# An attention and two-MLP kernel: half-height first score products, one cast moved to ScalarE, result stores on GpSimd's queue, and new planner numbers

## The chip, the cores and the metric

The kernel runs on one core of one Trainium2 chip. The metric is device time in microseconds (us), the median of several runs. Engines are named as the profile names them: PE (TensorE; PEld is its weight load), DVE (VectorE), ACT (ScalarE), POOL (GpSimd) and SP (SyncE, which here only issues transfers; "SPq" and "POOLq" are the queues on which these two engines issue DMAs).

## The reference

```python
scores = np.matmul(z, z.transpose(0, 2, 1)) / S          # B=2, S=3008, z is 64 wide
out = np.matmul(np.maximum(scores, 0.0) ** 2, v)
x = (u * out).reshape(B * S, 256)                         # attention result
h = x @ w_in                                              # first MLP, 256 -> 2048
g = (a0 + a1*h + a2*h**2 + a3*h**3) / (1 + |b0|*|h| + |b1|*h**2 + 1e-6)
x = g @ w_out                                             # 2048 -> 256
h = x @ w2_in                                             # second MLP
g = np.maximum(h, 0.0) + alpha * np.minimum(h, 0.0)
result = g @ w2_out
```

The weights arrive as 64-bit floats and are taken apart on the chip.

## The kernel before, in words

All products are made in a reduced 32-bit format, so each operand is split into a high half (a cast) and a low half (the original less the cast), and a product is two or three matmuls. The attention runs over 12 blocks (2 batches of 6 blocks of 512 queries, the last 448 wide) with 12 pairs of key tiles each. A score tile goes PE (`L912`) -> ACT (relu `L927`/`L935`, square `L940`, cast `ahi` `L463`) -> DVE (`alo` `L468`) -> PE (8 products `L963` with `ahi`, 4 products `L974` with `alo`). Score tiles are symmetric, so DVE also transposes some (`L824`), SP writes them to DRAM (`rt<-rt`) and reads them back for a later block (`rr<-rt`). At the end of a block (`a_end`) SP loads `ut`, DVE multiplies the accumulators with it (`L1007`), and the result goes to DRAM (`xd`, `L1013`), from where the first MLP reads it (`xr`, `L1064`).

Beside the attention DVE, ACT and POOL decode the 32 pieces of the weights (`weight`, tiles `wraw` and `dec`, DVE lines `L576` to `L657`), and the first 17 steps of the first MLP run. A step of the first MLP is 12 products (`L1034` to `L1036` into `h`), seven DVE operations (`L1093` to `L1105`) that make `ghi` and `glo`, and 12 products back (`L963`, `L974`). The second MLP has its hidden products into `m` or `h` and two DVE operations (`L1163`, `L468`) for each step.

No scheduler of the compiler is used. Every instruction is recorded as an operation of `Plan` with an assumed duration, and `Plan.order()` plays these through with a cost model: an engine takes the ready operation with the earliest due time, buffers come from numbered rooms, and the resulting order is written out. Each engine then works strictly in its order. The order of PE is the order of recording. The constants at the top (`PACE`, `SAME`, `SOONER`, `SAFE`, `AFTER`, `NEXT`, `DEBT`, `EDGE`, `R0`, `RD`, `SOON`, `FAR`) are the costs, horizons and pacing of this planner: `AFTER` and `SAFE` are how long after its issue a transfer is taken to land, `R0` and `RD` say at which attention steps the weight pieces are recorded, and `DEBT` and `EDGE` how much DVE work may be outstanding when one more is recorded. `WARM` is the number of matmuls on zeros before the first real one.

In the opening `load_z` makes `zA`: rows 0 to 63 hold the high half of z (the cast), rows 64 to 127 the low half (`L709`). `zB` has the halves the other way round. A score is `zA·zA` plus `zB·zA`. For the very first tile the two products are recorded apart, so that the first can run before `zB` is there.

## Time and profile before

| | |
|---|---|
| median of 3 runs | 1495.2 us (1494.6 to 1495.29) |
| the profiled execution's own time | 1494.43 us |
| its span, first to last instruction | 1492.6 us |
| PE busy | 1484.3 us, 99% |
| DVE busy | 1413.4 us, 95% |
| ACT busy | 1182.2 us, 79% |
| POOL busy | 80.8 us, 5% |

The span is what the trace covers; 1.8 us of the execution lie outside it. Shares are of the span. PE is busy almost throughout, so the time is the sum of PE's products and of the few places in which PE stands.

### The profile page before, as it was taken

The numbers are of one execution on the slowest core, as the hardware profiler recorded it, in microseconds if no ns is written. First come the engines' busy times: TensorE is split into PE (matmuls) and PEld (weight loads), VectorE is DVE, ScalarE is ACT, GpSimd is POOL, SyncE is SP. The second block draws the span as 40 slices with busy tenths as digits, with TensorE's granted clock in tenths as the row PEclk, the third lists the DMA queues.
The fourth block names the chain that finished last, engine by engine and source line by source line (L and its number), as shares of the span: only waits on it lengthen the run. The fifth ranks groups of instructions, "written<-read, shape, count | busy, mean of one in ns | idle before, by whom it ended". The sixth has DMA issues, their size and how long they took to land.

```text
span 1492.6 us, 18002 instructions
## 1 busy us (share of the span) xinstructions
PE 1484.3 (99%) x6655; PEld 1242.4 (83%) x6655; DVE 1413.4 (95%) x1459; ACT 1182.2 (79%) x1403; POOL 80.8 (5%) x98
## 2 busy tenths in 40 slices
PE   9999999999999999999999999999999999999999
PEld 7888888888887888888888888888888888888988
DVE  8899999999999999999999999989999999999953
ACT  8888868887877868797788778778887888788844
POOL 1000000011122330000000000000000000000000
PEclk9999999999999999999999999999999999999999
DMA  6998677668996863000000000000000000000000
GB/s 199 236 247 212 192 212 237 160 164 230 251 263 214 288 224 123 19 29 15 29 29 29 29 14 29 15 29 29 29 29 14 29 15 29 29 25 29 15 1 25
DMA packets 195145, 149.77 MB, mean 100 GB/s; under 512 B 154336, under 2 KB 166128, under 8 KB 195056
## 3 DMA queue, kind: packets, MB, share of 16 engines
q1 hardware_dynamic: 185424, 114.00, 27.6%
q0 software_dynamic: 9632, 34.62, 7.1%
q8 instruction: 52, 0.85, 0.2%
q14 instruction: 37, 0.30, 0.1%
HBM read 86.52 MB, written 59.24 MB: 98 GB/s over the span
## 4 chain that ended last, share of the span: by engine, by line
PE 91%; DVE 6%; issue 1%; DMA 1%; ACT 0%; DVEq 0%; ACTq 0%
PE acc L963 36%; PE acc L974 18%; PE h L1036 6%; PE h L1035 6%; PE h L1034 6%; PE m L1036 5%; PE m L1035 5%; PE m L1034 5%; PE s L912 3%; PE acc L953 1%; PE h L912 1%; DVE alo L468 1%; DVE glo L1105 0%; DMA rr<-rt 0%; DVE ghi L1102 0%
## 5 line engine op out<-in xcount | busy, mean ns | idle before, releaser
L963 PE MATMUL acc<-ghi,w 128*128 128x512 f32 (+1 forms) x1472 | 360.7, 387 | 0.0
L963 PEld LDWEIGHTS acc<-ghi,w 128*128 128x128 f32 x1472 | 275.6, 188 | 54.9
L963 PE MATMUL acc<-ahi,vt 128*128 128x512 f32 (+1 forms) x1152 | 281.1, 386 | 1.2 <-DVE ahi L856 1.0
L963 PEld LDWEIGHTS acc<-ahi,vt 128*128 128x128 f32 x1152 | 215.1, 188 | 43.0 <-DVE ahi L856 1.4
L1090 ACT ACTIVATE t<-h,sc 128x1024 f32<-128x1024 f32 (+1 forms) x96 | 114.2, 1190 | 137.8 <-PE h L1036 133.9
L974 PE MATMUL acc<-glo,w 128*128 128x512 f32 (+1 forms) x736 | 195.2, 387 | 0.4 <-DVE glo L1105 0.4
L974 PEld LDWEIGHTS acc<-glo,w 128*128 128x128 f32 x736 | 137.8, 188 | 28.4 <-DVE glo L1105 0.8
L1034 PE MATMUL h<-xhi,w 128*128 128x512 f32 (+1 forms) x412 | 157.8, 383 | 0.3 <-ACT sq L1088 0.3
L1036 PE MATMUL h<-xhi,w 128*128 128x512 f32 (+1 forms) x412 | 157.7, 383 | 0.0
L1035 PE MATMUL h<-xlo,w 128*128 128x512 f32 (+1 forms) x412 | 157.7, 383 | 0.0
L974 PE MATMUL acc<-alo,vt 128*128 128x512 f32 (+1 forms) x552 | 146.5, 385 | 0.0
L1034 PE MATMUL m<-xhi,w 128*128 128x512 f32 (+1 forms) x356 | 137.7, 387 | 1.0 <-DVE m L1163 1.0
L1035 PE MATMUL m<-xlo,w 128*128 128x512 f32 (+1 forms) x356 | 137.6, 387 | 0.0
L1036 PE MATMUL m<-xhi,w 128*128 128x512 f32 (+1 forms) x356 | 137.6, 387 | 0.0
L1157 ACT ACTIVATE m<-m,sc 128x512 f32<-128x512 f32 (+1 forms) x178 | 116.0, 693 | 22.4 <-PE m L1036 21.0
L1093 DVE SCALAR_TENSOR_TENSOR ab<-sq,cb,ab 128x1024 f32<-128x1024 f32 (+1 forms) x96 | 120.8, 1258 | 11.4 <-ACT sq L1088 11.0
L468 DVE TENSOR_TENSOR glo<-m,ghi 128x1024 fp32r<-128x1024 f32 (+1 forms) x96 | 114.8, 1196 | 10.8 <-ACT ghi L463 10.8
L1098 ACT ACTIVATE sq<-ab,one 128x1024 f32<-128x1024 f32 (+1 forms) x96 | 110.7, 1153 | 13.1 <-DVE t L1095 12.9
L974 PEld LDWEIGHTS acc<-alo,vt 128*128 128x128 f32 x552 | 103.6, 188 | 19.3
L1163 DVE TENSOR_TENSOR m<-m 128x1024 f32<-128x1024 f32 (+1 forms) x89 | 107.2, 1205 | 11.0 <-ACT m L1157 10.9
L1102 DVE TENSOR_TENSOR ghi<-t,sq 128x1024 fp32r<-128x1024 f32 (+1 forms) x96 | 114.8, 1195 | 2.5 <-ACT sq L1099 2.4
L1105 DVE TENSOR_TENSOR glo<-t,sq 128x1024 fp32r<-128x1024 f32 (+1 forms) x96 | 114.9, 1197 | 1.6
(100 smaller groups left out, 2640.1 us busy)
## 6 DMA issues: line engine op xcount, KB each, us to landing
rt<-rt SPq DMA_DIRECT2D x200, 128.0 KB, 3.6
rr<-rt SPq DMA_DIRECT2D x40, 512.0 KB, 5.6
rr<-rt SPq DMA_DIRECT2D x20, 448.0 KB, 5.9
wraw<-in_moe_w_in_dram POOLq DMA_DIRECT2D x16, 512.0 KB, 5.7
wraw<-in_moe_w_out_dram POOLq DMA_DIRECT2D x16, 512.0 KB, 5.8
wd<-dec POOLq DMA_DIRECT2D x16, 512.0 KB, 3.9
w<-wd POOLq DMA_DIRECT2D x16, 512.0 KB, 5.9
x2d<-x SPq DMA_DIRECT2D x11, 512.0 KB, 2.6
```

What stands on the lines that cost most here:

```text
L468: lambda: nc.vector.tensor_tensor(lo(), src(), hi().bitcast(F32), ALU.subtract),
L963: nc.tensor.matmul(acc()[:, e, :n], w()[:, k, i, e * P : (e + 1) * P], hi()[:, i, :n], start=first and i == 0 and k == 0, stop=False,)
L974: nc.tensor.matmul(acc()[:, e, :n], w()[:, 0, i, e * P : (e + 1) * P], lo()[:, i, :n], start=False, stop=last and i == both - 1,)
L1034: nc.tensor.matmul(acc, w_hi, hi, start=first, stop=False)
L1035: nc.tensor.matmul(acc, w_hi, lo, start=False, stop=False)
L1036: nc.tensor.matmul(acc, w_lo, hi, start=False, stop=last)
L1090: act(N, lambda: activation(c(t), c(h), AF.Identity, scale=a3, bias=a2), [h], [t], psum=True, ptr=2, **kw)
L1093: dve(N, lambda: stt(c(ab), c(sq), b1, c(ab), ALU.mult, ALU.add), [sq, ab], [ab], ptr=1, **kw)
L1098: act(N, lambda: activation(c(sq), c(ab), AF.Abs_reciprocal_sqrt, bias=one), [ab], [sq], ptr=1, **kw)
L1102: dve(N, lambda: tt(c(hi), c(t), c(sq), ALU.mult), [t, sq], [hi], **kw)
L1105: dve(N, lambda: tt(c(lo), c(t), c(sq), ALU.mult), [t, sq], [lo], **kw)
L1157: lambda i=i, f=f: nc.scalar.activation(t()[:, i, :n], h()[:, i, :n], AF.Copy, scale=al[:, f : f + 1]),
```

## The change

The first score product of the first two key pairs of block (0, 0) takes only rows 0 to 63 (high half times high half; the product of the two low halves is left out for these two pairs), and is recorded as needing only that part. The second pair's products are recorded in four pieces too. The cast of the second z group moves from DVE to ACT. The store of `xd` moves from SP's queue to GpSimd's. One matmul on zeros goes, and the planner's numbers change, so that the order on DVE, ACT, SP and POOL changes in many places.

```diff
-PACE = 25.0
-SAME = 0.16
-SOONER = 30.0
+PACE = 22
+SAME = 0.13
+SOONER = 38
 WIRE = 0.6
-SAFE = 1.0
+SAFE = 1.5
-AFTER = 4.0
-FIRST, NEXT = 5, 4
-FILL, DEBT, EDGE = 0.97, 4.0, 3.0
+AFTER = 5
+FIRST, NEXT = 5, 6
+FILL, DEBT, EDGE = 0.97, 3, 4
-R0, RD = 3, 3
-WARM = 7
+R0, RD = 1, 2.5
+WARM = 6
-NEAR, SOON, FAR = 25.0, 10.0, 40.0
+NEAR, SOON, FAR = 25.0, 12, 50
@@ load_z
-        dve(m, lambda: nc.vector.tensor_copy(t()[:, 0:m], raw()[:, 0:m]), [raw], [t], fast=True)
+        if (b, g) == (0, 1):
+            act(m, lambda: nc.scalar.copy(t()[:, 0:m], raw()[:, 0:m]), [raw], [t])
+        else:
+            dve(m, lambda: nc.vector.tensor_copy(t()[:, 0:m], raw()[:, 0:m]), [raw], [t], fast=True)
@@ load_z, zB of the first group: the two halves are recorded apart
-            act(m, lambda: nc.scalar.copy(q()[HALF:P, 0:m], raw()[HALF:P, 0:m]), [raw], [q])
+            act(m, lambda: nc.scalar.copy(q()[HALF:P, 0:m], raw()[HALF:P, 0:m]), [raw], [(q, 1)])
@@ a_scores
-                nc.tensor.matmul(o, keys, (zA, zB)[k][b, j]()[:, q0:n], start=k == 0, stop=k == 1)
-        opening = (b, j, kp) == (0, 0, 0)
+                h = slice(0, HALF if opening and k == 0 else P)
+                nc.tensor.matmul(o, keys[h], (zA, zB)[k][b, j]()[h, q0:n], start=k == 0, stop=k == 1)
+        opening = (b, j) == (0, 0) and kp in order[b, j][:2]
-                pe(n, 1, lambda i=i: mm(i, (0,)), [zk, zA[b, j]], [hs[i]])
+                pe(n, 1, lambda i=i: mm(i, (0,)), [(zk, 0), (zA[b, j], 0)], [hs[i]])
@@ a_end
-        sp(n, lambda: nc.sync.dma_start(out=d()[:, :, :n], in_=t()[:, :, :n]), [t], [d])
+        pool_dma(
+            n,
+            lambda: nc.gpsimd.dma_start(out=d()[:, :, :n], in_=t()[:, :, :n]),
+            [t], [d], level="load", rate=210.0, horizon=SOON,
+        )
```

What the change does to the order is read from the instructions of the two built programs. First DVE's opening, before (`zA` is made for three z groups in turn, `zB` for the first):

```order
L706 CAST zA<-zraw 128x512
L709 TENSOR_TENSOR zA<-zraw,zA 64x512
L706 CAST zA<-zraw 128x512
L722 TENSOR_TENSOR zB<-zraw,zA 64x512
L709 TENSOR_TENSOR zA<-zraw,zA 64x512
L706 CAST zA<-zraw 128x512
L709 TENSOR_TENSOR zA<-zraw,zA 64x512
```

and of the change (three lines lower in the file):

```order
L709 CAST zA<-zraw 128x512
L712 TENSOR_TENSOR zA<-zraw,zA 64x512
L725 TENSOR_TENSOR zB<-zraw,zA 64x512
L712 TENSOR_TENSOR zA<-zraw,zA 64x512
L709 CAST zA<-zraw 128x512
L712 TENSOR_TENSOR zA<-zraw,zA 64x512
```

The cast of the second group no longer stands ahead of `zB`. It stands on ACT, behind the cast for `zB` and ahead of the first relu.

Second, SP's queue around the first load of `ut`, before (`rt` are pieces of transposed score tiles on their way to DRAM):

```order
L871 DMA rr<-rt_0_1_100 128x1024
L838 DMA rt_0_3_102<-rt 32x16x64 x8
L838 DMA rt_0_4_103<-rt 32x16x64 x8
L998 DMA ut<-in_u_dram 128x2x512
L838 DMA rt_0_5_104<-rt 32x16x64 x4
```

and of the change:

```order
L874 DMA rr<-rt_0_1_100 128x1024
L841 DMA rt_0_3_102<-rt 32x16x64 x4
L754 DMA zB<-zA 64x512 x2
L841 DMA rt_0_3_102<-rt 32x16x64 x4
L841 DMA rt_0_4_103<-rt 32x16x64 x4
L1002 DMA ut<-in_u_dram 128x2x512
L841 DMA rt_0_4_103<-rt 32x16x64 x4
```

Between the `rr` load and the `ut` load stood 16 transfers, and now stand 14.

Third, DVE at the end of the attention, where the last `ut` multiply (448 wide) stands, before:

```order
L614 TENSOR_TENSOR dec<-dec,sr_83 128x256 x2
L603 SCALAR_TENSOR_TENSOR dec<-wraw,dec 128x512
L1095 TENSOR_TENSOR t<-t,sq 128x1024
L635 TENSOR_TENSOR dec<-dec 128x512
L608 TENSOR_TENSOR dec<-dec 128x512
L1007 TENSOR_TENSOR ut<-acc_81,ut 128x2x448
L1163 TENSOR_TENSOR m<-m 128x1024
```

and of the change (lines above `L1012` are 4 lower, those below 12):

```order
L1105 SCALAR_TENSOR_TENSOR ab<-sq,cb,ab 128x1024
L1107 TENSOR_TENSOR t<-t,sq 128x1024
L657 SCALAR_TENSOR_TENSOR dec<-dec,sg 128x256
L468 TENSOR_TENSOR xlo<-xr,xhi 128x512
L657 SCALAR_TENSOR_TENSOR dec<-dec,sg 128x256
L468 TENSOR_TENSOR xlo<-xr,xhi 128x512
L1108 TENSOR_TENSOR t<-t,c_4926 128x1024
L1011 TENSOR_TENSOR ut<-acc_81,ut 128x2x448
```

The last multiply stands further ahead, and part of the decoding that stood before it now stands behind it.

## Rows read from the trace of the kernel before

**Rows 1.** The page: busy time of each engine, share of the span, instructions.

```profile
PE 1484.3 (99%) x6655; PEld 1242.4 (83%) x6655; DVE 1413.4 (95%) x1459; ACT 1182.2 (79%) x1403; POOL 80.8 (5%) x98
```

**Rows 2.** Windows: stretch, its length, each engine's busy time (instructions), clock, DMA.

```profile
400.00:500.00 100.00, 99.00 (x440) 81.57 (x439) 96.77 (x126) 75.53 (x95) 24.52 (x24) 1.00 0.86 250
500.00:600.00 100.00, 98.19 (x446) 83.08 (x445) 99.88 (x115) 76.66 (x93) 26.30 (x30) 1.00 0.59 197
```

**Rows 3.** Waits of PE: for what, us in total, times, longest.

```profile
PE m L1034 <- DVE m L1163: 1.0, 1, 1.0
PE acc L963 <- DVE ahi L856: 1.0, 1, 1.0
PE acc L974 <- DVE glo L1105: 0.4, 1, 0.4
PE h L1034 <- ACT sq L1088: 0.3, 1, 0.3
```

**Rows 4.** Timeline of PE, 548 to 556 us: start, us, what, idle before.

```profile
548.88 0.39 PE L1036 MATMUL h<-xhi,w 128*128 128x512 f32 x1
550.32 0.50 PE L1034 MATMUL m<-xhi,w 128*128 128x512 f32 x1 [1.05 <-DVE m L1163]
550.65 0.40 PE L1035 MATMUL m<-xlo,w 128*128 128x512 f32 x1
...
555.89 0.39 PE L1034 MATMUL h<-xhi,w 128*128 128x512 f32 x1
```

**Rows 5.** Timeline of DVE, 547 to 556 us.

```profile
547.45 0.68 DVE L608 TENSOR_TENSOR dec<-dec 128x512 f32<-128x512 f32 x1
548.05 1.08 DVE L1007 TENSOR_TENSOR ut<-acc,ut 128x896 f32<-128x896 f32 x1
...
550.19 1.21 DVE L1096 TENSOR_TENSOR t<-t,c 128x1024 f32<-128x1024 f32 x1
551.32 0.47 DVE L657 SCALAR_TENSOR_TENSOR dec<-dec,sg 128x256 fp32r<-128x256 f32 x1
551.71 1.21 DVE L468 TENSOR_TENSOR glo<-m,ghi 128x1024 fp32r<-128x1024 f32 x1
...
554.38 1.28 DVE L468 TENSOR_TENSOR xlo<-xr,xhi 128x512 fp32r<-128x512 f32 x2
```

**Rows 6.** Timeline of the opening, DVE, ACT and PE.

```profile
4.71 0.43 DVE L706 CAST zA<-zraw 128x512 fp32r<-128x512 f32 x1
...
5.05 0.68 DVE L722 TENSOR_TENSOR zB<-zraw,zA 64x512 fp32r<-64x512 f32 x1
...
5.88 0.72 PE L912 MATMUL s<-zB,zA 128*128 128x512 f32 x2 [0.41 <-DVE zB L722]
...
6.40 1.09 ACT L927 ACTIVATE r<-s 128x512 f32<-128x512 f32 x2 [2.25 <-PE s L912]
```

**Rows 7.** Timeline of DVE and SP: the first load and multiply of `ut`.

```profile
40.38 13.41 SPq L838 DMA_DIRECT2D rt<-rt  x16
53.89 0.55 SPq L998 DMA_DIRECT2D ut<-in_u_dram  x1
59.43 1.22 DVE L1007 TENSOR_TENSOR ut<-acc,ut 128x1024 f32<-128x1024 f32 x1 [4.14 <-PE acc L974]
```

**Rows 8.** Timeline of PE and DVE: the fourth and the ninth multiply.

```profile
183.08 1.07 PE L974 MATMUL acc<-alo,vt 128*128 128x512 f32 x4
184.56 1.22 DVE L1007 TENSOR_TENSOR ut<-acc,ut 128x1024 f32<-128x1024 f32 x1
402.12 1.23 DVE L1007 TENSOR_TENSOR ut<-acc,ut 128x1024 f32<-128x1024 f32 x1 [1.19 <-PE acc L974]
```

**Rows 9.** Waits of SP's queue, and transfers by kind (count, KB each, us to landing).

```profile
SPq L1013 <- DVE ut L1007: 64.0, 7, 23.7
wd<-dec POOLq DMA_DIRECT2D x16, 512.0 KB, 3.9
xd<-ut SPq DMA_DIRECT2D x10, 512.0 KB, 4.3
```

More of the change, by code (lines that the diff above doesn't have):

```diff
@@ L725, in load_z @@
                 [raw, (t, 0)],
-                [q],
+                [(q, 0)],
             )
@@ L1012, in a_end @@
         xd[b, j] = d
-        sp(n, lambda: nc.sync.dma_start(out=d()[:, :, :n], in_=t()[:, :, :n]), [t], [d])
+        pool_dma(
+            n,
+            lambda: nc.gpsimd.dma_start(out=d()[:, :, :n], in_=t()[:, :, :n]),
+            [t],
+            [d],
+            level="load",
+            rate=210.0,
+            horizon=SOON,
+        )
     def split_x(src, sr, n, make, psum=False):
```

## The prediction

> **What bounds the kernel now.** I read the page first: PE is busy for 1484.3 of 1492.6 us [rows 1], so the time is PE's products plus what PE waits, and a change that alters no product's size can win at most those waits. The windows say where they are: 400:500 and 500:600 lack 1.00 and 1.81 us [rows 2]; from 600 us to the end every stretch is full. The list of PE's waits names the largest: 1.0 and 1.0 us for DVE, 0.4 for DVE and 0.3 for ACT [rows 3]. These figures are too small, because a matmul's modelled end overlaps the next start. From start to start, matmuls of 512 columns follow each other 0.23 us apart; the wait at 548.88 makes it 1.44, and the next step is 0.33 [rows 4]. So a wait that the row calls 1.05 costs 1.21 + 0.11 = 1.3 us. Taken so, the waits of [rows 3] cost 1.3, 1.3, 0.7 and 0.6 us, and what lies before them in the trace (one of 0.5 behind a `ut` multiply, four of 0.1) brings the sum to **4.8 us** between 185 and 564 us. The opening is apart: there PE stands until 5.88 us for `zB` [rows 6].
>
> The reader is then to see why PE waits: DVE is 99.88% busy in 500:600 [rows 2], and the product at 555.89 starts 0.23 us after the `xlo` that it reads has ended, the last of a stretch without gaps on DVE [rows 4, 5]. In this stretch PE's place in time is DVE's. Whatever DVE loses earlier (idle time), PE pays here.
>
> **The change, part by part.**
>
> *Opening.* With the cast of the second z group gone from DVE, `zB` follows 0.34 us earlier (4.71 to 5.05) [rows 6], the second pair of products and ACT's chain behind it (6.40 on) too. ACT has room for the cast: it is idle for 2.25 us before 6.40 [rows 6], against 0.54 us for each of the two 512-wide relus that follow. The first products can start one matmul on zeros earlier, but what follows still waits for `zB`, so the seventh is not won a second time. No row shows a matmul with 64 rows; between nothing and the 0.23 us of a full one I take the full one, since the columns are the same; the four of them then lie in the wait for `zB`, which covers them. If they cost less, that wait hides it. The part is worth **-0.34 us** where ACT's chain leads, and is contained in the DVE sum below.
>
> *DVE's work ahead of the stretch that binds.* I follow the one product at 555.89, the first of the third 512-token group of the first MLP. By the two orders, DVE has 648 instructions up to its `xlo` in both kernels: now four more of 1.13 us (`L1102`, `L1103`, `L1104`, `L1163`; as 550.19 to 551.32), one z cast of 0.34, one `L608` of 0.60 and two `L657` of 0.39 fewer [rows 5, 6]. That is 4.52 - 0.34 - 0.60 - 0.78 = **+2.8 us** ahead of it. PE has one hidden step of the second MLP more in front of it, 12 x 0.227 = 2.7 us, so 2.7 us less are left behind it. By work alone the end moves by +0.1 us: the shuffle of the order on DVE is no gain in itself.
>
> *DVE's idle time ahead of it.* Here the transfers matter.
> - First `ut`. DVE stood 4.14 us before 59.43. The row names PE, but PE's last product of the block had ended at 52.06, so it was the load, issued at 53.89 and 5.5 us on its way [rows 7]. In the new order 14 transfers instead of 16 stand between the `rr` load and this one, at 13.41/16 = 0.84 us each [rows 7]: it lands 1.7 us earlier. DVE has one transpose more and one cast fewer ahead of it (+0.8 us), so it arrives 0.8 us later. The idle time falls from 4.14 to 1.6: **-2.5 us**. Bounds: 0, if the queue is held up elsewhere, and -4.14.
> - Ninth `ut`: DVE waits 1.19 us for PE now [rows 8], and has 1.3 us more work ahead: **-1.2 us**.
> - Fourth and seventh `ut`: DVE comes 0.41 us after PE's last product at the fourth (184.56, and 183.08 + 1.07) [rows 8] and at once at the seventh. By the orders it has 1.8 and 1.5 us less work ahead, PE 0.4 less (the matmul on zeros), so DVE now waits about 1.0 us at each: **+2.0 us**. Bounds: 0 to +2.0.
> - The other gaps (waits for ACT in the middle) I take as unchanged, with 2 us either way.
>
> Sum -1.7 us. The bounds add up to -4.1 - 1.2 - 2 = -7.3 (more than PE has to give, which is rival A) and -1.2 + 2.0 + 2 = +2.8.
>
> *Behind that product.* The wait of 0.4 in [rows 3] (`L974` for `glo`, at 563.72; cost 0.7) should go: by the orders DVE has 8 us less ahead of that `glo` relative to PE. **-0.7 us.**
>
> *Stores on GpSimd's queue.* Twelve leave SP, where the queue stood 64.0 us behind this instruction in 7 waits [rows 9]; what stood behind it were `rt` and `rr` transfers, whose lateness is in the idle times above. On POOL the same wait for the multiply stands ahead of weight loads. In the order the first store stands behind two weight loads, the second and third behind six. The first reader of `xd`, a load for the first MLP, stood ten rows behind the store in SP's order, with four loads and some thirty transfers between, so the store itself costs nothing.
>
> A store by this queue is not dearer in the rows: `wd` of 512 KB lands in 3.9 us from POOL, `xd` of 512 KB in 4.3 us from SP [rows 9]. The Trainium skill speaks against it: "SBUF — State Buffer", section "SBUF: two separate sides", says that DMAs issued from GpSimd need descriptors written by GpSimd, which is locked out while DVE runs an instruction in its two-port mode, and advises SP or ACT. By that rule each store would start up to one fast DVE operation later, an estimate of 12 x 0.4 us of lateness on the queue and nothing on PE; by the rows, nothing at all. The trace does not show it.
>
> **Sum:** +0.1 - 1.7 - 0.7 = **-2.3 us**. Against the profiled execution's own 1494.43 us that is 1492.1; its span is 1492.6 with 1.8 us around it. The median of the runs stands 0.8 us above that execution, so I forecast **1492.9 us**.
>
> **The rivals.**
>
> A. *All waits go.* If DVE loses its idle time of 59.43 entirely and the fourth and seventh `ut` bring no new wait, DVE is 4 to 5 us earlier, all 4.8 us of PE's waits vanish, and the opening gives its 0.34: 1495.2 - 5.1 = 1490.1. For it speaks that lateness in this stretch has one source, that the planner now takes transfers to land 1.5 us later than before (`AFTER` and `SAFE`), so it puts fewer DVE instructions in front of data that is not there, and that the last multiply and a good part of the decoding behind it have changed places. Against it: the waits that vanish bring PE forward against a DVE that is still full.
>
> B. *Nothing moves.* The early `ut` load is held up behind another transfer (the DMA engines are busy for 0.86 of 400:500 [rows 2]), idle time only changes place, and +0.1 - 0.7 is left: 1494.6.
>
> C. *Slower.* A store that waits for its multiply on POOL holds up the weight loads behind it. SP stood up to 23.7 us behind the same instruction [rows 9]. If two weights are decoded that much later, their DVE work (seven to eight instructions each, 3.6 us from start to start by the pitches of [rows 5]) falls into 500:600, where DVE has 0.1 us free [rows 2]: +7.2 - 2.3 gives 1500. It decides against the change from 5.3 us of decoding pushed there, that is from the second late weight. Against it: the planner puts few stores ahead of loads, and POOL is busy 5% of the span [rows 1].
>
> **How the numbers follow.** My forecast (DVE 1 to 4 us earlier at 555.89, time 1491.8 to 1494.2) 0.38; A 0.33; B 0.18; C 0.11. A measurement of this kernel can tell a change of about 0.2%, 3.0 us, from none: faster is below 1492.2, slower above 1498.2. Faster: A and a small part of the forecast, 0.38. Same: the rest of the forecast and B, 0.51. Slower: C, 0.11. The range leaves out C and the far end of A: 1489.6 to 1496.8, which above 1494.6 takes in most of the +2.8 us by which DVE's idle time may grow. The likeliest case alone is 1491.8 to 1494.2.
>
> **What would show it.** In the trace after: `zB` on DVE starts near 4.7 instead of 5.05, and ACT's first relu near 6.05 instead of 6.40. The idle time before the first `ut` multiply is 1 to 2 us instead of 4.14; about 1 us stands before the fourth and the seventh. The list of PE's waits keeps one or two for DVE between 470 and 560 us, with a sum near 1.5 instead of 2.9 us, and none at the `glo` near 564. DVE stays at 99% in 500:600. The forecast is wrong if PE is full in 400:600 (then A), if the waits are as long as before (B: a DVE idle time that I took as unchanged has grown), or if POOL's weight loads come later than before and the decoding ends later (C). It is also wrong if a wait appears before 60 us, where DVE has up to 3 us more work ahead of some products and PE's margin is thin.

## The result, and the profile after

The changed kernel takes 1502.2 us (median of 4 runs, 1500.1 to 1503.6), the kernel before 1494.9 in the same session: ratio 1.0051 [1.0038, 1.0063], **slower by 0.5%**, 7.3 us. The forecast was 1492.9 with a range up to 1496.8.

The busy line of the page after answers to [rows 1]:

```profile
PE 1489.6 (99%) x6654; PEld 1243.9 (83%) x6654; DVE 1411.4 (94%) x1458; ACT 1182.7 (79%) x1405; POOL 87.9 (6%) x110
```

DVE and ACT did the same work as before to within 2 us. PE is "busy" for 5 us longer with one instruction fewer: some of its matmuls took longer. The span grew from 1492.6 to 1500.1 us. PE's waits after, against [rows 3] (for what, us in total, times, longest):

```profile
PE acc L967 <- DVE ut L1011: 2.3, 2, 1.8
PE s L455 <- DVE one L437: 1.4, 1, 1.4
PE acc L978 <- DVE alo L468: 1.2, 2, 0.7
PE h L916 <- ACT sq L1100: 0.7, 1, 0.7
PE m L1046 <- DVE m L1175: 0.5, 1, 0.5
PE h L1047 <- DVE xlo L468: 0.2, 1, 0.2
```

The waits for `glo` and `ahi` and the one of `L1034` for `sq` are gone, and the one in front of `m` is half as long. New, or longer, are the waits for `ut`, for `alo`, for an `h` that a score pair is to fill and, at 565 us, for `xlo` (0.2 in the row, but 1.0 us from start to start). Where they stand decides; three places make most of the 7.5 us by which the span grew.

**The opening.** Timeline of PE in the changed kernel:

```profile
1.44 2.93 PE L455 MATMUL s<-wz 128*128 128x512 f32 x6 [1.44 <-DVE one L437]
4.30 1.22 PE L916 MATMUL s<-zA 64*128 64x512 f32 x2
5.45 1.22 PE L916 MATMUL s<-zB,zA 128*128 128x512 f32 x2
...
11.76 0.63 PE L916 MATMUL h<-zB,zA 128*128 128x512 f32 x1
12.18 0.61 PE L916 MATMUL acc<-zA 128*128 128x512 f32 x1
12.61 0.42 PE L916 MATMUL acc<-zB,zA 128*128 128x512 f32 x1
12.87 0.39 PE L916 MATMUL acc<-zA 128*128 128x512 f32 x1
13.10 0.39 PE L916 MATMUL acc<-zB,zA 128*128 128x512 f32 x1
13.33 2.00 PE L967 MATMUL acc<-ahi,vt 128*128 128x512 f32 x8
```

Read the starts: 11.76, 12.18, 12.61 are 0.43 us apart, which for 512 columns is the 1.2 GHz level; from 12.87 on they are 0.23 apart, the 2.4 GHz level. PE had no gap since 1.44 us. In the kernel before the same matmuls were already 0.23 us apart at 6.85 us:

```profile
6.85 0.39 PE L912 MATMUL acc<-zB,zA 128*128 128x512 f32 x1
7.08 0.39 PE L912 MATMUL acc<-zA 128*128 128x512 f32 x1
...
10.59 1.77 PE L963 MATMUL acc<-ahi,vt 128*128 128x512 f32 x7
```

The first product of `ahi` comes at 13.33 instead of 10.59: 2.7 us. Not all of it is the level of the clock: the eight products of the first two pairs stand 0.57 us apart (4.30 to 5.45 for two), the later ones at the same level 0.43, which makes about 1 us of the 2.7.

**139 us.** Timeline of PE and ACT in the changed kernel:

```profile
135.37 0.39 PE L1048 MATMUL h<-xhi,w 128*128 128x512 f32 x1
...
135.80 1.21 ACT L1102 ACTIVATE t<-h,sc 128x1024 f32<-128x1024 f32 x1
...
138.35 1.07 PE L978 MATMUL acc<-alo,vt 128*128 128x512 f32 x4
139.00 1.02 ACT L1100 ACTIVATE sq<-h 128x1024 f32<-128x1024 f32 x1
...
140.08 0.51 PE L916 MATMUL h<-zA 128*128 128x512 f32 x1 [0.66 <-ACT sq L1100]
```

A step of the first MLP has filled `h` until 135.6; ACT reads it four times, the last until 140.02; but 16 matmuls (3.6 us) behind the step stands a score pair that goes into the same `h`. PE waits for ACT. In PE's order before, no score pair in `h` stands between the second and the third step. The next wait, at 142.68, is for the third `ut`.

**318 us**, the seventh `ut`. Timeline of SP's queue, ACT, DVE and PE in the changed kernel:

```profile
296.54 12.10 SPq L841 DMA_DIRECT2D rt<-rt  x14
308.75 0.43 SPq L874 DMA_DIRECT2D rr<-rt  x1
...
314.43 1.06 ACT L463 CAST ahi<-rr 128x1024 fp32r<-128x1024 f32 x1 [2.10 <-DMA rr<-rt]
...
317.43 1.23 DVE L468 TENSOR_TENSOR alo<-r,ahi 128x1024 fp32r<-128x1024 f32 x1 [2.09 <-ACT ahi L463]
...
318.57 1.22 DVE L1011 TENSOR_TENSOR ut<-acc,ut 128x1024 f32<-128x1024 f32 x1
...
319.84 0.96 PE L967 MATMUL acc<-ahi,vt 128*128 128x512 f32 x3 [1.79 <-DVE ut L1011]
```

This is a chain of four waits: an `rr` load issued behind 14 `rt` stores, ACT's cast behind the load, DVE behind ACT, PE behind DVE. In the kernel before the same load was issued behind six `rt` stores fewer, 6.8 us earlier, and DVE came to `ut` 6.7 us earlier:

```profile
301.99 0.42 SPq L871 DMA_DIRECT2D rr<-rt  x1
...
311.86 1.23 DVE L1007 TENSOR_TENSOR ut<-acc,ut 128x1024 f32<-128x1024 f32 x1
```

PE's own order has a part in both waits for `ut`. Timeline of PE in the kernel before, behind the seventh block:

```profile
310.75 1.07 PE L974 MATMUL acc<-alo,vt 128*128 128x512 f32 x4
311.65 0.39 PE L1034 MATMUL h<-xhi,w 128*128 128x512 f32 x1
```

The 12 products of the eighth step, and 12 products back behind them, stand there between the block's last product and the next block's first, so that PE has work while DVE multiplies; behind the third block the second step does the same, at 133.98 us. In the changed kernel the second step stands 16 matmuls earlier and the eighth comes only at 332.7 us, and at both places PE has eight score products alone before it needs what DVE is to set free.

Start to start, the waits at 139, 142 and 318 us cost 0.8, 0.6 and 2.0 us; with the opening's 2.7, some 0.7 between 450 and 500 us and 0.6 behind the last product that is the difference to within a microsecond.

One number follows DVE through all kernels of this study: its idle time between 20 and 550 us, which is 530 less its busy time in the windows view (the third busy time of the row). The rows of the kernel before and of the changed kernel:

```profile
20.00:550.00 530.00, 527.74 (x2365) 441.53 (x2363) 511.40 (x627) 430.44 (x551) 72.44 (x78) 1.00 0.80 221
```

```profile
20.00:550.00 530.00, 525.90 (x2351) 438.95 (x2350) 502.55 (x614) 424.61 (x543) 81.47 (x94) 1.00 0.81 222
```

18.6 us before, 27.5 after. Idle time of DVE can be a consequence of PE's waits as well as a cause; it is used here as a ledger, not as a proof. (The expectations count it from the start to the twelfth `ut` instead: 23.1 us before, 32.5 in the changed kernel.)

### The profile page after: what moved, and what is told of

The parts are those of the page before. It is cut to its first block, busy times and chain, and to the rows that moved or that the text cites. A ratio compares the mean times of both kernels' runs of the same rounds, so it can differ in the third digit from the quotient of the medians.

```text
span 1500.1 us, 18114 instructions
## 1 busy us (share of the span) xinstructions
PE 1489.6 (99%) x6654; PEld 1243.9 (83%) x6654; DVE 1411.4 (94%) x1458; ACT 1182.7 (79%) x1405; POOL 87.9 (6%) x110
## 4 chain that ended last, share of the span: by engine, by line
PE 62%; DVE 1%; DMA 0%; issue 0%; POOL 0%; ACT 0%; POOLq 0%
PE acc L967 20%; PE acc L978 10%; PE m L1046 5%; PE m L1048 5%; PE m L1047 5%; PE h L1047 5%; PE h L1048 5%; PE h L1046 5%; PE acc L957 1%; DMA w<-wd 0%; DVE m L1175 0%; DVE xlo L468 0%; DVE dec L603 0%; DVE t L1108 0%; POOL w L674 0%
## 5 line engine op out<-in xcount | busy, mean ns | idle before, releaser
L1169 ACT ACTIVATE m<-m,sc 128x512 f32<-128x512 f32 (+1 forms) x178 | 112.5, 692 | 16.9 <-PE m L1048 16.6
L1115 DVE SCALAR_TENSOR_TENSOR ab<-ab,ghi 128x1024 f32<-128x1024 f32 (+1 forms) x96 | 114.8, 1196 | 0.9
L1108 DVE TENSOR_TENSOR t<-t,c 128x1024 f32<-128x1024 f32 (+1 forms) x96 | 114.7, 1195 | 0.5
```

The lines of the kernel that those rows point to most:

```text
L1108: dve(N, lambda: tt(c(t), c(t), c(c1), ALU.add), [t, c1], [t], **kw)
L1115: dve(N, lambda: stt(c(ab), c(ab), ONE, c(hi).bitcast(F32), ALU.add, ALU.mult), [ab, hi], [ab], **kw)
L1169: lambda i=i, f=f: nc.scalar.activation(t()[:, i, :n], h()[:, i, :n], AF.Copy, scale=al[:, f : f + 1]),
```

## The experiments

Eighteen kernels beside the two. "Idle" is the ledger number just defined. "Steps" are the places in PE's order at which the third, fourth and seventh step of the first MLP begin, counted in matmuls; the matmuls on zeros and the products back into `acc` are counted, the hidden products of the first MLP are not.

| kernel | median us | ratio to before | idle us | steps |
|---|---|---|---|---|
| before | 1494.2 to 1494.9 | | 18.6 | 646, 708, 1188 |
| changed | 1502.2 | 1.0051 [1.0038, 1.0063] | 27.5 | 617, 723, 1219 |
| e1 seven zeros | 1505.6 | 1.0073 [1.0060, 1.0086] | 33.2 | 618, 724, 1220 |
| e2 full rows | 1504.0 | 1.0063 [1.0050, 1.0076] | 28.7 | as changed |
| e3 old numbers | 1506.9 | 1.0092 [1.0077, 1.0108] | 30.5 | 633, 695, 1171 |
| e4 new numbers alone | 1501.9 | 1.0047 [1.0034, 1.0059] | 25.4 | 618, 724, 1220 |
| e5 store alone | 1494.3 | 1.0001 [0.9992, 1.0010] | 19.2 | as before |
| e6 opening alone | 1508.1 | 1.0093 [1.0078, 1.0107] | 31.8 | 633, 695, 1171 |
| e7 recording numbers | 1506.2 | 1.0082 [1.0069, 1.0096] | 35.4 | 618, 724, 1220 |
| e8 cost numbers | 1499.4 | 1.0033 [1.0022, 1.0044] | 23.0 | as before |
| e9 order of before | 1496.8 | 1.0012 [1.0004, 1.0021] | 19.7 | 645, 707, 1187 |
| e10 neutral nudge | 1494.0 | 0.9999 [0.9990, 1.0008] | 19.0 | as before |
| e11 no second `ut` load | 1499.5 | 1.0037 [1.0024, 1.0049] | 24.5 | as changed |
| e12 cast re-planned | 1506.3 | 1.0082 [1.0068, 1.0096] | 31.4 | 634, 696, 1172 |
| r13 cast, steps kept | 1494.8 | 1.0003 [0.9994, 1.0012] | 20.5 | as before |
| r14 steps moved alone | 1502.7 | 1.0060 [1.0048, 1.0072] | 31.0 | 634, 696, 1172 |
| r15 edits, old numbers, steps kept | 1496.8 | 1.0015 [1.0006, 1.0024] | 20.6 | 645, 707, 1187 |
| r16 `DEBT`, `EDGE` alone | 1506.8 | 1.0084 [1.0071, 1.0098] | 28.0 | 618, 724, 1220 |
| r17 changed, steps of before | 1503.2 | 1.0063 [1.0048, 1.0079] | 23.0 | 645, 707, 1187 |
| r18 `AFTER`, `SAFE` alone | 1497.0 | 1.0019 [1.0011, 1.0028] | 22.2 | as before |

(Where the opening's first pair is issued with one matmul on zeros fewer, the counts are lower by one.)

### The opening's clock: e1 and e2

```diff
-        for i in range(WARM):
+        for i in range(WARM + 1):        # e1: seven issued, order of the changed kernel
```
```diff
-                h = slice(0, HALF if opening and k == 0 else P)
+                h = slice(0, P)          # e2: all 128 rows, order of the changed kernel
```

> The changed kernel with seven matmuls on zeros in place of six; every engine's order is that of the changed kernel. In the changed kernel PE's matmuls of 512 columns follow each other 0.43 us apart until 12.6 us, in the kernel before only until about 4.4 us (then 0.23). Theory 1 (the missing seventh matmul on zeros leaves PE at the low clock for longer): the pitch falls to 0.23 us near 6 us at the latest, the first product of line 967 starts near 10.6 instead of 13.3 us, and the time falls from 1502.2 by 2.7 to about 1499.5 us. Theory 2 (the half-height products or the order behind them keep the clock low): the pitch stays at 0.43 us until about 12.6 us, and the time is 1502.2 to 1502.6. Rival on the net: the clock comes early but the later waits (317 us and others) grow by what PE has won, and the time stays near 1502.

> The changed kernel with the four half-height products made over all 128 rows again (the product of the low halves is back in them); the order is that of the changed kernel, six matmuls on zeros. Theory 2 (64 rows are what keeps the clock low): the pitch falls to 0.23 us near 6 us, the first product of line 967 starts near 10.7 us and the time falls to about 1499.5 us. Theory 1 (one matmul on zeros fewer): the pitch stays at 0.43 us until 12 us or so and the time is 1502. If both edits are needed for the late clock, this kernel and the one with seven matmuls both have the early clock.

With seven matmuls on zeros the pitch stayed at 0.43 us until 11.0 us, so theory 1 fell; but the time, 1505.6, was 3 us above what theory 2 said. With 128 rows the pitch fell at 7.3 us; timeline of PE in e2:

```profile
5.65 1.05 PE L916 MATMUL s<-zB,zA 128*128 128x512 f32 x2
6.50 1.01 PE L916 MATMUL acc<-zA 128*128 128x512 f32 x2
7.34 0.63 PE L916 MATMUL acc<-zB,zA 128*128 128x512 f32 x2
7.82 0.39 PE L916 MATMUL s<-zA 128*128 128x512 f32 x1
...
10.61 2.01 PE L967 MATMUL acc<-ahi,vt 128*128 128x512 f32 x8
```

So the half-height products may have to do with it; one trace of each does not decide it (e11 below has the opening of the changed kernel, and there the clock rose at 5.1 us). The products themselves stand closer too: 0.43 us apart at the lower level (5.65 to 6.50 for two) instead of 0.57. But the time did not come down, as the rival on the net had said. What PE won at the opening it lost at 139 us, where the wait grew from 0.7 to 3.2 us (waits of PE in e2):

```profile
PE h L916 <- ACT sq L1100: 3.2, 1, 3.2
```

It lost more than it had won: the product behind that wait came at 141.74 us, against 140.08 in the changed kernel. DVE was later too. It had waited 4.06 us for the load of the second `ut` (2.80 in the changed kernel) and came to that multiply at 102.14 us instead of 100.44. e1 has the same wait of 3.2 us with a late clock, and its second `ut` came at 103.61 us. So this wait follows how late DVE comes to the second `ut`, as well as how early PE comes.

### The parts one by one: e3 to e8

e3 is the changed kernel with the old planner numbers (six zeros); e4 is the kernel before with the new numbers alone; e5 and e6 are before with only the store, and only the opening's edits; e7 and e8 divide e4's numbers:

```diff
 e7
-FIRST, NEXT = 5, 4
+FIRST, NEXT = 5, 6
-FILL, DEBT, EDGE = 0.97, 4.0, 3.0
+FILL, DEBT, EDGE = 0.97, 3, 4
-R0, RD = 3, 3
+R0, RD = 1, 2.5
 e8
-PACE = 25.0
+PACE = 22
-SAME = 0.16
+SAME = 0.13
...
```

> The changed kernel with all the planner's numbers of the kernel before, but six matmuls on zeros; the opening's edits and the stores on GpSimd's queue stay. Theory (the new numbers, by the order that they give, cause the waits at 139, 142 and 317 us, 4 us together): those waits go, only the late clock (2.7 us) is left, and the time is about 1497.5 us. Rival (the stores on GpSimd's queue cause them, since DVE's ut multiply and the weight loads now meet there): the waits near a ut multiply stay, and the time is 1501 to 1502.

> The kernel before with the planner's new numbers alone; full-height products, the cast on DVE, seven matmuls on zeros and the stores on SP's queue stay. Theory (the new numbers cost the 4 us of waits): clock early as before, waits of PE near 140 and 318 us, time about 1499 us. Rival (the opening and the stores carry the loss): no such wait, time 1494.5 to 1495.5 us.

> The kernel before with only the stores of the row results on GpSimd's queue; the planner's numbers and the opening are those of before, and the planner lays out the order anew. Theory (order): the store itself costs nothing, and what it changes comes through a new order in which DVE stands idle in other places; the total idle time of DVE ahead of the twelfth ut multiply (23.1 us before, 32.5 in the changed kernel) tells the time: by 1 us of PE's waits for each 2 us of it. Before with this one edit gives 1495 to 1503 us, and the landing time of the store is 4 to 6 us. Rival (queue): weight loads behind a store on GpSimd's queue come late; then DVE's idle time ends with POOL or a weight load, and the decoding ends later than in the kernel before. Rival (nothing): 1494.5, no matter what the order does.

> The kernel before with only the opening's edits: half-height first products, the cast of the second z group on ScalarE, six matmuls on zeros; the planner lays out the order anew. By the four kernels that ran, half-height products hold the clock at the lower level until 10 to 12.6 us (full-height: 4.4 to 7.1), and PE's lost time there (2 to 2.7 us) came back at a later wait. Theory (order): the clock rises late, PE is 1 to 2.5 us behind before at 15 us, but the time is set by DVE's idle time in the new order: 1496 to 1503 us. Rival (the late clock is paid in full and nothing else changes): 1494.5 + 2.2 = 1496.7 us with DVE's idle time ahead of the twelfth ut at 23 us.

> The kernel before with the new values of NEXT, DEBT, EDGE, R0 and RD alone: the numbers that say when weight pieces and steps of the first MLP are recorded, so PE's order changes. Theory (a step of the first MLP ahead of 140 us is what DVE and ScalarE cannot serve in time): the wait of h behind sq near 139 us is here too, about 1 us or more, and the time is 1497 to 1500. Rival (the costs and horizons do it): no wait near 139 us and 1494.5 to 1496.

> The kernel before with the new values of PACE, SAME, SOONER, SAFE, AFTER, SOON and FAR alone: the costs and horizons of the planner; PE's order is that of before. Theory (a transfer taken to be longer draws the rt stores in front of the rr loads): in the changed kernel the rr load ahead of the seventh ut was issued at 308.75 us behind 14 rt stores, in the kernel before at 301.99 ahead of them; here it comes behind them too, DVE waits for ScalarE's cast near 315 us, PE for ut near 318, and the time is 1496 to 1499. Rival (the recording numbers do it): the waits are those of before, 1494.5 to 1496.

e4 carries the whole loss of the changed kernel (its trace, 1499.1 us, is the fastest of its five runs), so the numbers were blamed rightly; but e3 and e6 show that the opening's edits with the *old* numbers are dearer still (12 to 14 us, where e3 was expected to lose 3 and e6 at most 9), and not by the clock: in e6 the pitch fell already at 5.2 us. The store alone costs nothing, as the last of its rivals had said; the planner laid out nearly the old order for it (in the trace 29 of DVE's rows stand elsewhere, the first at 414 us), so the theory on a new order was hardly tried. e7's wait of `h` behind `sq` near 137 us came, with 4.5 us, and the loss (11.7) was above what was expected. e8 lost 4.9 us, a little more than the theory said, but in other places: its waits stand at 460 and 553 us (2.1 and 2.2 us in the trace), none near 318, so the place was wrong. The parts do not add up: 0 + 13.6 + 7.3 against 7.3 together.

### What in the opening's edits: e9, e12, r13, r14

e9 issues the opening's edits where the instructions of before stood (nothing recorded differently, so each engine's order is that of before, the second pair's products too). e12 records only the cast on ScalarE and lets the planner lay out the order.

```diff
 e9: recorded as before, issued otherwise
-        dve(m, lambda: nc.vector.tensor_copy(t()[:, 0:m], raw()[:, 0:m]), [raw], [t], fast=True)
+        def cast():
+            if (b, g) == (0, 1):
+                nc.scalar.copy(t()[:, 0:m], raw()[:, 0:m])
+            else:
+                nc.vector.tensor_copy(t()[:, 0:m], raw()[:, 0:m])
+        dve(m, cast, [raw], [t], fast=True)
```

> The kernel before with the opening's edits put in where the instructions stood: the planner records what it recorded before, so every engine keeps the order of the kernel before, but six matmuls on zeros are issued, the first products of the first two key pairs take 64 rows, and the cast of the second z group is issued on ScalarE at the place that the plan gave it. Theory (order): the opening's edits cost and gain nothing by themselves; the time is 1493.5 to 1495.5 us and DVE's idle time ahead of the twelfth ut is 22 to 24.5 us, although the re-planned kernel with the same edits took 1508.1 us with 36.1 us of idle time. Rival (the edits themselves): a late clock or ScalarE's cast delays what follows, and the time is 1497 us or more with the order unchanged.

> The kernel before with only the cast of the second z group recorded on ScalarE, and the order laid out anew; full-height products, seven matmuls on zeros, the numbers of before. By the order SP now issues four rt transfers more ahead of the first ut load (20 behind the first rr load, as in the kernel with the whole opening, where DVE waited 7.4 us for that load). Theory (order): one cast moved is enough; DVE's idle time before the first ut is 7 us, ahead of the twelfth ut 30 us or more, and the time is 1499 to 1508 us. Rival (the half-height products or the split of the second pair do it): 1494 to 1496 us.

One cast of 0.4 us recorded on another engine costs 12 us; issued on the other engine without a new order, together with the half-height products, about 2 (e9's 1496.8 lies between its theory, at most 1495.5, and its rival, 1497 or more). In e12 the four additional `rt` transfers ahead of the first `ut` load and 7.9 us of DVE's idle time there were as expected, and looked like the cause. Two more kernels take the two halves of e12 apart. The places of the first MLP's steps are fixed while the program is recorded, from a running sum: `Plan.add` adds each DVE duration to `plan.debt` and takes off 0.97 of each PE duration (down to 0), and a step or a weight piece is recorded only while `plan.debt < DEBT + (EDGE if edge else 0)`. A cast that leaves DVE takes 0.335 us out of this sum.

```diff
 r13: e12, and
             act(m, lambda: nc.scalar.copy(t()[:, 0:m], raw()[:, 0:m]), [raw], [t])
+            plan.debt += m / 1920 + 0.068
 r14: the kernel before, and
         dve(m, lambda: nc.vector.tensor_copy(t()[:, 0:m], raw()[:, 0:m]), [raw], [t], fast=True)
+        if (b, g) == (0, 1):
+            plan.debt -= m / 1920 + 0.068
```

> The kernel before with the cast of the second z group recorded on ScalarE and the order laid out anew, as in the run with the cast alone (1506.3 us), but its 0.35 us are still counted as outstanding DVE work: by the orders the steps of the first MLP stand in PE's order where they stood before, while 20 instead of 16 rt transfers still stand between the first rr load and the first ut load. Theory P (PE's places of the steps are the loss): 1494 to 1497 us, the waits near 315, 383 and 395 us are gone, and DVE's longer wait for the first ut (7.9 instead of 4.1 us) is made up by the fourth ut at 184.5 us. Theory T (the late ut load and the transfers are the loss): the wait of 3.4 us near 119 us stays and the time is 1500 to 1506 us.

> The kernel before with 0.35 us taken off the outstanding DVE work at the opening and nothing else: no instruction moves to another engine, the cast stays on DVE, 16 rt transfers stand ahead of the first ut load as before, but three steps of the first MLP (the third, fourth and seventh) are recorded 12 to 16 matmuls earlier in PE's order, as in the run with the cast alone. Theory P: 1500 to 1506 us, with waits near 315 and 383 us, and none near 119 us. Theory T: 1494 to 1496 us.

The two halves come apart. r13 has the late `ut` load of e12, but the steps of before, and no loss. Timeline of SP's queue and DVE in r13, against [rows 7]:

```profile
40.08 16.76 SPq L842 DMA_DIRECT2D rt<-rt  x20
56.88 1.03 SPq L1002 DMA_DIRECT2D ut<-in_u_dram  x1
...
63.08 1.23 DVE L1011 TENSOR_TENSOR ut<-acc,ut 128x1024 f32<-128x1024 f32 x1 [7.59 <-DMA ut<-in_u_dram]
...
185.40 1.23 DVE L1011 TENSOR_TENSOR ut<-acc,ut 128x1024 f32<-128x1024 f32 x1
```

DVE is 3.65 us late at the first `ut` and 0.84 us late at the fourth (184.56 in [rows 8]): it made up the rest in what had been idle time, and PE has no new wait before 231 us. So a new order on DVE from the opening on, with PE's order kept, lost nothing. r14 moves no instruction to another engine, keeps the `ut` load where it was, and loses 8 us. Waits of PE in r14, the timeline of PE at the eighth step, and that of DVE before it:

```profile
PE s L914 <- ACT r L929: 2.6, 1, 2.6
PE h L1036 <- ACT w L463: 1.6, 1, 1.6
PE h L1038 <- DVE w L468: 1.5, 1, 1.5
```

```profile
314.34 0.50 PE L1036 MATMUL h<-xhi,w 128*128 128x512 f32 x1 [1.61 <-ACT w L463]
...
316.54 0.79 PE L1038 MATMUL h<-xhi,w 128*128 128x512 f32 x1 [1.47 <-DVE w L468]
```

```profile
297.44 1.29 DVE L1095 SCALAR_TENSOR_TENSOR ab<-sq,cb,ab 128x1024 f32<-128x1024 f32 x1 [2.46 <-ACT sq L1090]
...
302.72 0.42 DVE L576 TENSOR_SCALAR dec<-wraw 128x512 f32<-128x512 f32 x1
...
315.84 0.65 DVE L468 TENSOR_TENSOR w<-dec,w 128x512 fp32r<-128x512 f32 x1
```

PE does not pay at a step that moved. The seventh stands 16 matmuls (3.6 us) earlier, at 283.38 us, and waits for nothing. The eighth, at 314.34, has its place of before, but the weight `w` that it multiplies with is not decoded yet: PE waits for its high half on ACT and then for its low half on DVE, which came at 315.84 us, against 307.83 in the kernel before. DVE's first operations for the seventh step, for which it had stood 2.46 us behind ACT, are now ahead of that weight's decoding (302.72, against 294.05 before). Theory P holds for this edit by the time and by the waits at 315 and 383 us. It does not say all: 1.05 us was lost near 119 us too, where PE's order is still that of before (it differs from 154 us on, DVE's from 108). The running sum moves weight pieces as well as steps.

### Is every new order a loss? e10

```diff
-SAME = 0.16
+SAME = 0.155
```

> The kernel before with one planner number moved by 3% (SAME 0.16 to 0.155): no instruction added or moved to another engine, PE's order the same, some 700 rows of DVE in other places. Theory (order): the kernel before stands at a good order among many, and a neutral nudge loses time: DVE's idle time ahead of the twelfth ut rises above 24 us, and the time to 1495.5 to 1502 us. Rival (only the edits of meaning cost time): 1494.0 to 1495.2 us and 23 us of idle time.

The theory fell here: some 700 rows of DVE change places and nothing is lost. PE's order is the same. But in the trace DVE's order is that of before until 348 us, so this kernel says nothing of the places before 320 us at which the changed kernel loses; r13, whose order on DVE differs from the opening on, does. By both, an order that differs on DVE is not in itself worse.

### The waits of the changed kernel: e11, r16, r17

e11 leaves out the load of the second `ut` (its multiply reads a tile of `v`). r16 sets `DEBT` and `EDGE` alone in the kernel before. r17 is the changed kernel with the old `DEBT` and `EDGE` and the line of r13.

```diff
 e11
-            lambda: nc.sync.dma_start(
+            lambda: (b, j) != (0, 1) and nc.sync.dma_start(
 r16, on the kernel before
-FILL, DEBT, EDGE = 0.97, 4.0, 3.0
+FILL, DEBT, EDGE = 0.97, 3, 4
```

> The changed kernel, in its own order, with the load of the second ut left out; the multiply of that block reads a tile of v that is already there, so its result is another one. In the changed kernel DVE waited 2.8 us for this load at 100 us. Theory (DVE's waits for transfers are what PE pays): DVE comes to the third ut (141.41 us in the changed kernel) 2 to 3 us earlier, PE's waits at 139.9 and 142 us (1.7 us together) go, and the time falls by 1 to 3 us to about 1500. Rival (the idle time only moves to the next wait, for ScalarE or for the rr loads): DVE's idle time ahead of the seventh ut stays at 25 us, and the time at 1502.

> The kernel before with the new DEBT and EDGE alone (3 and 4 in place of 4 and 3): PE's order differs, the first step of the first MLP comes after 492 attention matmuls instead of 508, the eighth after 1354 instead of 1290, and DVE has 36 instead of 42 decoding instructions behind it at the third ut. Theory P: this alone does what all five recording numbers did (1506.2 us): a wait of h behind sq near 137 us and 1501 to 1508 us. Rival (NEXT or R0 and RD do it; by the orders R0 and RD change no row at all): 1494 to 1496 us.

> The changed kernel with the old DEBT and EDGE, and the moved cast still counted as outstanding DVE work: PE's order has the steps of the first MLP where the kernel before has them; the opening's edits, the stores on GpSimd's queue and all other new numbers stay. Theory P: the waits at 139, 142 and 318 us are gone, what is left is the loss of the cost numbers (5 us) and the opening's (0 to 2 us), and the time is 1496 to 1500 us. Theory T, or a late clock paid in full: 1501 to 1504 us.

e11 is not decided for either side. The time fell by 2.7 us and DVE came to the third `ut` 2.4 us earlier, as the theory said; but the waits of 0.7 us for `h` and of 2.1 us for `ut` stayed, and in this trace the clock rose at 5.1 instead of 12.6 us, which alone puts PE 2.4 us ahead. r16 did what was expected: two numbers carry the whole of e7. r17 missed: the waits at 139, 142 and 318 us are gone, so the steps' places did make them, and DVE's idle time fell from 27.5 to 23.0 us, but the time is no better; it lies where the rival put it, though in its trace the clock rose early (4.6 us). Its waits, and two stretches of its windows view (length, busy time of PE, PEld, DVE, ACT, POOL, granted clock, DMA share, GB/s):

```profile
PE s L917 <- ACT r L932: 3.2, 4, 2.4
PE m L1047 <- DVE m L1176: 1.9, 1, 1.9
```

```profile
500.00:505.30 5.30, 5.30 (x26) 4.68 (x25) 5.30 (x7) 2.70 (x4) 2.19 (x3) 1.00 1.05 395
509.80:513.20 3.40, 3.40 (x11) 3.04 (x10) 3.22 (x3) 3.40 (x6) 1.04 (x2) 0.50 0.64 186
```

PE waited 2.4 us at 505 us; then the granted clock was 0.50, the 1.2 GHz level, for 3.4 us, so a matmul took twice as long and another 1.7 us went. The same came behind the wait at 554 us. Waits and clock make 8 us. These waits come with the new numbers that r17 keeps: r15 below, with the old ones, has neither, and e8, with the cost numbers alone, has one at 553 us too. By the window from 500 us DVE is full there; why its order is late is not shown.

### What is left: r15 and r18

r15 is e3 with the line of r13: all edits, old numbers, steps kept. r18 is the kernel before with the new `AFTER` and `SAFE` alone.

> The changed kernel with all the planner's old numbers, six matmuls on zeros, the opening's edits and the stores on GpSimd's queue, and the moved cast still counted as outstanding DVE work, so that the steps of the first MLP stand where the kernel before has them. Theory P: 1494 to 1497 us, against 1506.9 us for the same kernel without that count; DVE's idle time ahead of the twelfth ut 24 to 26 us instead of 36.3. Theory T (the two queues with the opening lose together): above 1499 us.

> The kernel before with the new AFTER and SAFE alone (transfers taken to land 1.5 us later); PE's order is that of before, 20 instead of 16 rt transfers stand ahead of the first ut load. Theory L (these two numbers are the loss of the cost numbers, 5 us, since rt stores become due earlier and the loads behind them come later): 1497 to 1501 us with DVE's idle time ahead of the twelfth ut at 26 us or more. Rival (PACE, SAME, SOON and FAR are, and DVE makes up a late first ut by the fourth): 1494 to 1495.5 us.

r15 is 10 us faster than e3, as theory P said, by one line that moves no instruction between engines. What remains of the edits is 2.2 us, like e9's 1.8. In the trace of r15 the clock rose at 12.6 us and the run took 1496.8; in that of e9 it rose at 4.4 us and the run took 1494.9. The eleven times of e9 lie in two groups, 1492.7 to 1494.9 (4 runs) and 1496.3 to 1498.1 (7). It fits that the remaining 2 us are the late clock; when the clock rose in the runs that were only timed is not known, so this is argued and not shown. r18 gives 2.8 of e8's 4.9 us, at the lower edge of what its theory said.

## Why the prediction was wrong, point by point

- **Opening, -0.34.** `zB` started at 4.60 us on DVE (4.7 said), the first relu on ACT at 6.28 (6.05 said, 6.40 before). The step that failed is that the half-height products "lie in the wait for `zB`, which covers them". In the changed kernel's trace PE has no wait for `zB` left to cover anything: the products of the first two pairs stand 0.57 us apart, where the forecast took 0.23 for one, and the clock rose at 12.6 us. Together that is 2.7 us of PE. Whether that reaches the end depends on what follows: in e2 full rows gave it back and the wait at 139 us took it; in e9 and r15, where that wait does not follow, some 2 us remained.
- **DVE's work, +0.1.** The count of work was right, and of no use. It followed one product at 555.89 us and compared what stands ahead of it; the loss was made on PE before 320 us, where a step of the first MLP had changed its place against the tiles, PSUM buffers and weights that it needs. That PE's order had changed was seen only as 12 more matmuls in front of that product. It came at 564.71 us, 8.8 us later. Of this 2.7 are those matmuls; the other 6.1 are about what PE had lost by 320 us (2.7 in the opening, 3.4 at the three waits), while the waits behind 320 us, where the forecast looked, cost about as much as before.
- **DVE's idle time, -1.7 (bounds -7.3 and +2.8).** This is the term that broke. The first `ut` did better than forecast: no idle time at all, instead of 4.14 us. But by the second it was given back. Timeline of DVE in the changed kernel:

```profile
56.42 1.22 DVE L1011 TENSOR_TENSOR ut<-acc,ut 128x1024 f32<-128x1024 f32 x1
...
100.44 1.23 DVE L1011 TENSOR_TENSOR ut<-acc,ut 128x1024 f32<-128x1024 f32 x1 [2.80 <-DMA ut<-in_u_dram]
```

  In the kernel before the second multiply started at 99.89: three microseconds won had become half a microsecond lost. "The other gaps I take as unchanged, with 2 us either way" was the wrong sentence. The gaps at the `ut` multiplies went from 6.2 to 2.8 us (the ninth's is gone, as forecast; the fourth and the seventh, forecast at 1.0 each, have none), but between 20 and 550 us idle time grew by 8.9 us in all, so the other gaps grew by 12.3. The prediction named such growth as a sign (under B), but bounded it at 2.
- **The wait at `glo`, -0.7.** Right, it is gone; but nothing is won by it, since PE waits for `xlo` 1.0 us at 565 us.
- **Stores, 0.** Right, by e5: 1.0001 [0.9992, 1.0010], and `xd` landed 4.0 us after its issue from GpSimd's queue there, against 4.3 from SP's [rows 9]. In the changed kernel it took 5.7 us, but so did `wd` grow on that queue, from 3.9 to 5.3. The rule of the Trainium skill ("SBUF — State Buffer", "SBUF: two separate sides") would make descriptors from GpSimd late; no run here shows a cost of it on PE.
- **Rival C** gave 1500, close to the time, and for the wrong reason. The seventh weight load did stand on POOL behind a store that had waited 40.3 us for its multiply, and came at 143.9 instead of 96.4 us, and DVE's last decoding operation came at 570.8 instead of 552.8 us; both are signs that it had named. But in e4, with the stores on SP's queue, they came at 131.1 and 568.8 us and the loss was the same; in e5, with the store on POOL, the load came at 104.5 without loss; and in r17 it came at 93.4 with about the same loss.

What is shown: an edit or a number that moves the first MLP's steps in PE's order, and the weight pieces with them (by the running sum), costs 8 to 12 us here (r14, r16, against r13, r15). The cost numbers cost 5 us with PE's order unchanged (e8), of which `AFTER` and `SAFE` alone make 2.8. For the changed kernel itself the cause is shown only in part. Its numbers alone cost all of the 7.3 us (e4), and its waits before 320 us go when the steps are put back (r17), but then others come and the time stays. What stays open is which single row of DVE's or ACT's order makes the waits at 505 and 554 us in r17, and why the new numbers, dear by themselves, leave the opening's edits less dear (1502.2) than the old numbers do (1506.9): both have the steps misplaced, in different places. No kernel of this study is measurably faster than before; e10, e5 and r13 equal it.

## What to carry to other kernels

Where a planner or a recorder sets the order, ask of each edit what it changes in the planner's inputs, not only on the engines: here a cast of 0.4 us changed a running sum and with it PE's own order. Compare the order of the engine that is the bound first. At each place where something has moved on it look at what that instruction needs (its weight, its PSUM buffer) and when that is ready, at what it had covered where it stood, and at the work that it draws forward on the other engines: in r14 it was the next step that waited. A ledger up to one late product does not see it. To price the edits apart from the order, issue them in the old order.

## What the runs showed of the hardware

**Half-height matmuls and the clock.** The rise from 1.2 to 2.4 GHz is read from the first clock record of a trace and from the pitch; ahead of that record the windows view shows a granted clock of 1.00, although products of 512 columns stand 0.43 us apart. Twelve traces with full-height first products had the rise at 4.4 to 7.3 us; of eight with half-height ones, four had it at 4.4 to 5.2 and four at 10.4 to 12.6 us, although PE had no gap from 1.44 us on. The Trainium skill ("TensorE: Matmul & The Clock Gate", "What's actually happening") says that activity releases the throttle. The traces agree that it rises while PE works, and add that behind products on 64 rows it can come 3 to 8 us later than in the twelve others; how much of that is the 64 rows and how much is chance from run to run, these few traces can't say.

**A wait costs twice.** In eight of the traces the granted clock fell to 0.50 in mid-kernel, each time during a wait of PE of 1.5 to 4.5 us or within 2 us behind one, for 3.4 us (6.8 in two places). Such a stretch of 3.4 us costs PE up to 1.7 us beside the wait itself. It did not always come: 17 waits of 1.5 to 3.4 us, one of 3.2 in e2 and one of 3.4 in e12 among them, were not followed by it. The same page of the Trainium skill ("HAM oscillation — how this bites in real kernels") tells of waits that throttle PE again; the traces agree. In the trace of r14 such stretches last 10.2 us together and took about 5 of the 11.8 us by which that run was longer than the one of [rows 1].
